# The first two units in the form of the later ones: gated linear attention and a gated feed-forward layer on one core

## The chip, the core and the metric

The kernel runs on one core of a Trainium2 chip. A core has five engines with a queue of its own each: TensorE for matrix products (PE in the rows; PEld are its weight loads, PEq its sequencer), VectorE (DVE), ScalarE (ACT), GpSimd (POOL) and SyncE (SP), which here issues nearly all transfers. An engine works through its queue in order, and engines wait for one another by semaphores. Matrix products land in PSUM, eight banks, from where VectorE or ScalarE bring them to SBUF. The metric is the device time of one execution in microseconds (us).

## The reference

```python
def _attn_ref(q, k, v, alpha):                      # (4, 8, 768, 48) each
    state = np.zeros((B, H, D, D))
    for t in range(S):
        state = alpha[:, :, t, :, None] * state + np.einsum('bhd,bhe->bhde', k[:, :, t], v[:, :, t])
        y[:, :, t] = np.einsum('bhd,bhde->bhe', q[:, :, t], state)
    return y

def _moe_ref(x, w_gate, w_val, w_out):              # x (3072, 384); weights 384x1536, 384x1536, 1536x384
    g = x @ w_gate
    silu = g * (1.0 / (1.0 + np.exp(-g)))
    return silu * (x @ w_val) @ w_out
```

x is the attention's y with its 8 heads of 48 side by side. The weights come as 64-bit floats.

## The kernel before

**Two streams of work share the engines.** The attention is cut into 16 units, each 192 tokens of one batch with all 8 heads (4 units to a batch); a unit is three chunks c of 64 tokens, and its heads stand as four pairs g, the even head of a pair (j = 0) on partitions 0 to 47 and the odd one on 64 to 111. The feed-forward runs in seven blocks of tokens with 12 steps f of 128 hidden columns each; block 0 needs units 0 and 1. Each weight piece (g, v or o of a step, 384 KB) is read from HBM once, in 20 groups (group 0 to 2 one piece, the others two), cut from 64 bits to a float32 in three steps (`w3v0`, `w3v1`, `w3v2` for group 3), rounded to a float16 (`w3a`) whose rest is a second float16 (`w3p`). A product is nine matmuls of 128x128 weights.

**A unit.** `p`, `T`, `ea`/`ek`/`cq` bring alpha, k and q in, turned on TensorE, for units 0 to 3. `G` (L501) is a scan over alpha from behind, `f` (L505, L508) one from the front, `mk` makes the scaled keys Gs and `q` the scaled queries X[:, 0]. `K.c` (L554) turns chunk c's keys on TensorE and `kc.c` (L558, L559) copies them to the tile K, one copy for each head of the pairs; for units 4 to 15 VectorE turns them instead (`kr`, L570). `S` makes the scores, `ma` (L695) masks them into X[:, 1], `ad.c` adds chunk c's k v product to the state, `de` (L724) scales the state for the next unit, `Y` makes the outputs from values, states and X, `yh` and `yl` (L803) round them to a pair of float16, `R` and `x` put them into the block's input. `vc` copies the values to a tile U. `z`, `ib`, `is`, `ik`, `im`, `iv` are fillings.

**Two forms.** For units 2 to 15, `scores_carry` interleaves scores (L623, diagonal quarters of the 128x128 array) with the k v products of the chunks (L631, the other two quarters), `advance` adds them chunk by chunk with two instructions, one for each j (L718), and `outputs_quarters` (L754) makes the outputs in quarters. Units 0 and 1 (u < NST) use `scores`, then `carry` (L673), whose products run over all 128 rows and bring all three states out at once, since values (64 rows) and state (48 rows, on the other half) stand in one tile V of 96 columns to a pair, and the keys in K the same way, with an identity in chunk 0's state rows; `advance` then only copies (L709, L716, on ScalarE); `outputs` (L767 to L784) likewise mixes values and state in one product for two of four pairs.

**What sets the order.** ORDER, a string of some 1450 words `engine:step@banks`, is the program: each word issues one step on the named engine (t TensorE, v VectorE, s ScalarE, g GpSimd, y the transfers on SyncE), and each engine's queue is the words with its letter. Nothing reorders it.

Of the kernel before, what the change touches and what calls it, by code (L numbers as in the profile page):

```python
# [31 lines left out]
NST = 2  # L32
# [115 lines left out]
def main_path(ctx, tc, q, k, v, alpha, w_gate, w_val, w_out, out, flag, spill):  # L148
# [52 lines left out]
    DV = 2 * D  # L201
    Vt = [cp.tile([P, NU, G, DV], F32, name=f"V{i}") for i in range(NV)]
# [5 lines left out]
    nc.vector.memset(Vt[0], 0.0)  # L208
# [24 lines left out]
    VC = (slice(0, D), slice(D, DV))  # L233


    KC = (slice(0, D), slice(D, 2 * D))
    KW = NU * G * 2 * D
    Kt_ = [cp.tile([P, KW + 16], F32, name=f"K{i}") for i in range(NK)]
    Kt = [t_[:, 0:KW].rearrange("p (c g x) -> p c g x", c=NU, g=G) for t_ in Kt_]

    def keys_made():
        for t_ in Kt_:
            nc.gpsimd.memset(t_, 0.0)
        for t_ in Kt:
            for j in range(2):
                r = slice(j * BO, j * BO + D)
                nc.gpsimd.tensor_copy(out=t_[r, 0, :, KC[j]], in_=ident[r, r].unsqueeze(1).to_broadcast([D, G, D]))

# [269 lines left out]
    def qhat(u, eng):  # L518
# [12 lines left out]
    def q_odd(u, eng):  # L531
        X, r = state[u]["X"], slice(BO, BO + D)
        (eng.copy if eng is nc.scalar else eng.tensor_copy)(out=X[r, 1, 0:GF, :], in_=X[r, 0, 0:GF, :])

    def values_copied(u, eng):

        Vd = state[u]["V"]
        g0 = 0 if u >= NST else GF
        for j, r in ((0, slice(BO, P)), (1, slice(0, BO))):
            (eng.copy if eng is nc.scalar else eng.tensor_copy)(  # L540
                out=U[j * BO : j * BO + C, :, g0 * D : G * D].rearrange("p c (g e) -> p c g e", e=D),
                in_=Vd[r, :, g0:, VC[j]],
            )
# [37 lines left out]
    def scores(u, banks):  # L581

        st = state[u]
        KTt, X = st["Gs"], st["X"]
        st["S"] = [ps.tile([P, 512], F32, tag=banks[f], name=f"s{f}_{u}") for f in range(2)]
        st["sps"] = [t_[:, 0 : GF * T].rearrange("p (g t) -> p g t", g=GF) for t_ in st["S"]]
        for c in range(NU):
            cs = slice(1 + c * C, 1 + (c + 1) * C)
            cx = slice(c * C, (c + 1) * C)
            for g0 in range(GF):  # L590
                for f in range(2):
                    g = f * GF + g0
                    for j in range(2):
                        r, o = slice(j * BO, j * BO + D), (j if f else 1 - j) * BO
                        nc.tensor.matmul(
                            st["sps"][f][o : o + C, g0, cx], KTt[r, g, cs], X[r, 0, g, cx], start=True, stop=True
                        )

    def scores_carry(u, banks):
# [793 lines left out]
```

## Time and profile before

| | us |
|---|---|
| median of 3 runs | 515.17 (515.12 to 516.37) |
| the profiled execution | 514.84, span 513.1 |
| TensorE busy | 497.9 (97% of the span) |
| VectorE, ScalarE, GpSimd busy | 371.0, 285.3, 136.0 |
| transfers | 71.17 MB, mean 139 GB/s |

The span runs from the first to the last instruction; 1.7 us of the execution lie around it. Until about 34.5 us the core prepares units 0 and 1 and the first weights; from there feed-forward products follow one another on TensorE, with the later units between them, until the last output rows.

### The profile page before, as it was taken

The page shows a single profiled execution, that of the slowest core. Times are in us where ns is not written, and L with a number is a line of the kernel's source. Part 1 is how long each engine was busy: PE and PEld are TensorE (multiplying, and loading weights), DVE is VectorE, ACT ScalarE, POOL GpSimd, SP SyncE. Part 2 cuts the span into 40 slices and gives each one's busy share as a digit, 9 for nine tenths or more (in the row PEclk, how much of TensorE's full clock was granted, in tenths as well). Part 3 has the DMA queues.
Part 4 walks back from the last instruction along what each step waited for, and adds up shares of the span by engine and source line. Part 5 has one row for each costly group of instructions (what it writes and reads, how often), then busy time and mean ns, then how long its engine had stood idle before and what let it go on. Part 6 is the DMA issues. An engine that isn't in the chain of part 4 may idle for free.

```text
span 513.1 us, 13634 instructions
## 1 busy us (share of the span) xinstructions
PE 497.9 (97%) x5439; PEld 288.2 (56%) x5439; DVE 371.0 (72%) x617; ACT 285.3 (56%) x630; POOL 136.0 (27%) x152
## 2 busy tenths in 40 slices
PE   4999999999999999999999999999999999999995
PEld 4876666566666666655455554544554545456663
DVE  5999999999979989996978858936768334123123
ACT  5998998326431723333544425425317965589982
POOL 7544342235234322414214122121203100001100
PEclk9999999999999999999999999999999999999999
DMA  8999585555546444555655253453353624363521
GB/s 213 273 261 320 173 265 145 123 139 139 161 110 173 116 100 111 142 146 133 160 129 139 62 142 77 111 135 72 86 137 79 170 69 126 101 176 86 147 47 53
DMA packets 115143, 71.17 MB, mean 139 GB/s; under 512 B 64384, under 2 KB 112000, under 8 KB 115072
## 3 DMA queue, kind: packets, MB, share of 16 engines
q1 hardware_dynamic: 114368, 69.49, 51.3%
q8 instruction: 44, 0.72, 0.6%
q10 hardware_dynamic: 704, 0.74, 0.5%
q14 instruction: 27, 0.22, 0.1%
HBM read 61.34 MB, written 4.72 MB: 129 GB/s over the span
## 4 chain that ended last, share of the span: by engine, by line
PE 89%; DVE 4%; issue 2%; ACT 2%; DMA 1%; POOL 1%; SPq 0%; DVEq 0%; ACTq 0%; POOLq 0%
PE v L871 26%; PE g L871 26%; PE ops L953 14%; PE ops L958 13%; PE y L754 4%; PE s L623 2%; PE pt L448 1%; PE A L631 1%; DMA raw<-in_moe_w_val_dram 1%; DVE t L136 1%; DVE Gs L501 1%; DVE w L362 1%; PE kps L554 0%; DVE Gs L1067 0%; DVE h L887 0%
## 5 line engine op out<-in xcount | busy, mean ns | idle before, releaser
L871 PEld LDWEIGHTS <-w 128*128 128x128 f16 x1530 | 147.7, 98 | 131.8 <-issue 2.0
L871 PE MATMUL v<-xT,w 128*128 128x384 f16 (+2 forms) x765 | 154.1, 347 | 1.1 <-DVE h L885 0.7
L871 PE MATMUL g<-xT,w 128*128 128x384 f16 (+2 forms) x765 | 154.1, 347 | 0.3 <-ACT h L879 0.3
L899 POOL TENSOR_TENSOR hl<-h,hh 128x384 f16<-128x384 f32 (+1 forms) x54 | 63.3, 1176 | 245.8 <-ACT hh L893 238.4
L893 ACT CAST hh<-h 128x384 f16<-128x384 f32 (+1 forms) x84 | 46.1, 553 | 83.2 <-DVE h L887 43.5
L879 ACT ACTIVATE h<-g 128x384 f32<-128x384 f32 (+1 forms) x84 | 44.5, 530 | 84.5 <-PE g L871 84.4
L958 PE MATMUL ops<-w,hh 128*128 128x384 f16 x286 | 75.8, 326 | 0.0
L887 DVE TENSOR_TENSOR h<-h,v 128x384 f32<-128x384 f32 (+1 forms) x63 | 38.2, 607 | 51.3 <-PE v L871 42.6
L953 PE MATMUL ops<-hh,w 128*128 128x512 f16 x216 | 69.3, 379 | 0.0
L570 DVE STREAM_TRANSPOSE K<-Gs 32x384 f32<-32x384 f32 x96 | 54.7, 570 | 1.9
L953 PEld LDWEIGHTS <-w 128*128 128x128 f16 x324 | 31.4, 98 | 37.3
L958 PE MATMUL ops<-w,hl 128*128 128x384 f16 x143 | 46.6, 326 | 0.0
L899 DVE TENSOR_TENSOR hl<-h,hh 128x512 f16<-128x512 f32 (+1 forms) x30 | 19.4, 647 | 29.9 <-ACT hh L893 29.8
L953 PE MATMUL ops<-hl,w 128*128 128x512 f16 x108 | 40.9, 379 | 0.0
L958 PEld LDWEIGHTS <-hh 128*128 128x128 f16 x286 | 28.0, 98 | 18.4
L501 DVE TENSOR_TENSOR_SCAN Gs<-AT,Z 128x776 f32<-128x776 f32 x16 | 28.5, 1782 | 4.6 <-ACT AT L1041 4.4
L68 ACT ACTIVATE X<-y 112x384 f16<-112x384 f32 x28 | 12.8, 488 | 32.1 <-PE y L754 27.2
L527 POOL TENSOR_TENSOR X<-trq,AT 112x768 f32<-112x768 f32 x11 | 18.7, 1701 | 45.2 <-DMA V<-in_v_dram 13.2
L508 DVE TENSOR_TENSOR_SCAN AT<-AT,Z 128x774 f32<-128x774 f32 x16 | 30.0, 1877 | 0.6
L885 DVE SCALAR_TENSOR_TENSOR h<-v,h 128x384 f32<-128x384 f32 (+1 forms) x21 | 12.9, 612 | 19.5 <-PE v L871 17.5
L1070 POOL TENSOR_TENSOR Gs<-trk,Gs 128x768 f32<-128x768 f32 x10 | 16.8, 1683 | 32.5 <-DVE trk L423 32.4
L327 ACT ACTIVATE wc<-wc,wbias 128x384 f32<-128x384 f32 x36 | 23.4, 651 | 1.2
(155 smaller groups left out, 688.7 us busy)
## 6 DMA issues: line engine op xcount, KB each, us to landing
raw<-in_moe_w_gate_dram SPq DMA_DIRECT2D x12, 384.0 KB, 5.2
V<-in_v_dram SPq DMA_DIRECT2D x96, 48.0 KB, 3.6
raw<-in_moe_w_val_dram SPq DMA_DIRECT2D x12, 384.0 KB, 6.2
raw<-in_moe_w_out_dram SPq DMA_DIRECT2D x12, 384.0 KB, 5.9
wc<-in_moe_w_gate_dram SPq DMA_DIRECT2D x12, 384.0 KB, 4.1
wc<-in_moe_w_out_dram SPq DMA_DIRECT2D x12, 384.0 KB, 3.8
wc<-in_moe_w_val_dram SPq DMA_DIRECT2D x12, 384.0 KB, 3.8
L<-in_k_dram SPq DMA_DIRECT2D x24, 144.0 KB, 2.9
```

The lines of the kernel that those rows point to most:

```text
L327: nc.scalar.activation(dev, dev, AF.Relu, bias=wbias[:, 1:2], accum_out=wviol[:, 0, i : i + 1])
L501: nc.vector.tensor_tensor_scan(Gf[:, ::-1], Af[:, ::-1], Z[:, : 0 : -1], 0.0, op0=ALU.mult, op1=ALU.add)
L508: nc.vector.tensor_tensor_scan(Af, Af, Z[:, 1 : n + 1], Z[:, 0:1], op0=ALU.mult, op1=ALU.add)
L570: nc.vector.transpose(out=bass.AP(k0.tensor, k0.offset, [k0.ap[0], (G * 2 * D, NU), (2 * D, G), (1, 32)]), in_=Kg[j * BO + x : j * BO + x ...
L754: nc.tensor.matmul(to, w_, x_, start=(m == 0), stop=(m == 1))
L871: nc.tensor.matmul(pt, wsp[kind, f][a][:, kt * P : (kt + 1) * P], xT[blk][:, b_, kt, cs], start=(n == 0), stop=(n == 3 * KT - 1),)
L879: nc.scalar.activation(h, acc.pop(("g", blk, f)), AF.Silu, scale=(-1.0 if ("g", f) in negative else 1.0) / H_SCALE)
L887: nc.vector.tensor_tensor(out=h, in0=h, in1=v_, op=ALU.mult)
L893: (eng.copy if eng is nc.scalar else eng.tensor_copy)(out=hh, in_=acc["h", blk, f])
L899: eng.tensor_tensor(out=hl, in0=acc.pop(("h", blk, f)), in1=hh, op=ALU.subtract)
L953: nc.tensor.matmul(ops[blk][i], wsp["o", f][a][:, i * P : (i + 1) * P], h[b_], start=(first and n == 0), stop=(last and n == 2),)
L958: nc.tensor.matmul(ops[blk][i], h[b_][:, i * P : (i + 1) * P], wsp["o", f][a], start=(first and n == 0), stop=(last and n == 2),)
```

## The change

ORDER is new in its first third and the same, word for word, in its last 990 words. The special form of units 0 and 1 goes: `scores`, `carry`, `outputs`, `q_odd` and NST are deleted, and `scores_carry` and `outputs_quarters` serve all units. States get tiles St of their own, 112 rows by 48 columns to a pair, with the even head's state on rows 0 to 47 and the odd one's on 64 to 111, and V keeps only values, 48 columns to a pair. With this one instruction of 112 rows in `advance` and `decay` covers both heads of the pairs, in all units. K has 64 columns to a pair (48 of keys, 16 zeros), so that the k v product writes all 64 rows of a half. `k_turned` turns keys by eight plain products with the identity in two quarters of the array, instead of four transposes of 112 rows, and one copy brings them to K.

```diff
     def k_turned(u, c, bank):
-        kps = state[u]["kps", c] = ps.tile([C, G, 112], F32, tag=bank, name=f"kps{u}_{c}")
+        kps = state[u]["kps", c] = ps.tile([P, G, D], F32, tag=bank, name=f"kps{u}_{c}")
+        cs = slice(1 + c * C, 1 + (c + 1) * C)
         for g in range(G):
-            cs = slice(1 + c * C, 1 + (c + 1) * C)
-            nc.tensor.transpose(kps[:, g, :], state[u]["Gs"][0:112, g, cs], ident[0:112, 0:112])
+            for j in range(2):
+                r = slice(j * BO, j * BO + D)
+                nc.tensor.matmul(
+                    kps[(1 - j) * BO : (2 - j) * BO, g, :], state[u]["Gs"][r, g, cs], ident[r, r], start=True, stop=True
+                )
     def k_copied(u, c):
...
-        nc.scalar.copy(out=Ks[BO : BO + C, c, :, KC[0]], in_=kps[:, :, 0:D])
-        nc.scalar.copy(out=Ks[0:C, c, :, KC[1]], in_=kps[:, :, BO : BO + D])
+        nc.scalar.copy(out=Ks[:, c, :, 0:D], in_=kps)
...
-                            to[j * BO : j * BO + D], Ks[r, c, g, KC[j]], Vd[r, c, g, VC[j]], start=True, stop=True
+                            to[j * BO : (j + 1) * BO], Ks[r, c, g, :], Vd[r, c, g, :], start=True, stop=True
...
+    def advance(u, c, eng):
+
+        r, Sd = slice(0, 112), St[u % NV]
+        for gs, cps in state[u]["cps"][c]:
+            to = Sd[r, c + 1, gs] if c + 1 < NU else SE[r, gs]
+            if c == 0 and first_of_batch(u):
+                (eng.copy if eng is nc.scalar else eng.tensor_copy)(out=to, in_=cps[r])
+            else:
+                eng.tensor_tensor(out=to, in0=cps[r], in1=Sd[r, c, gs], op=ALU.add)
...
-                                w_, x_ = Vd[r, c, g, j * D : j * D + k], X[r, 0, g, cx]
+                                w_, x_ = Sd[r, c, g, :], X[r, 0, g, cx]
...
-        todo[f"S{u}"] = lambda eng, *banks: (scores if u < NST else scores_carry)(u, banks)
...
+        todo[f"S{u}"] = lambda eng, *banks: scores_carry(u, banks)
+        todo[f"Y{u}"] = lambda eng, *banks: outputs_quarters(u, banks)
```

In ORDER, beside this: the loads of unit 1's alpha and unit 0's q stand ahead of weight group 0's; unit 1's `q` moves from GpSimd to VectorE, two of the tile copies `p` and the second cutting steps of groups 1 to 4 from GpSimd to ScalarE, group 0's from ScalarE to GpSimd; the state additions of units 0 and 1 are new on VectorE but for the first, a copy on ScalarE.

VectorE's queue from unit 0's last masking to unit 1's first, before (Gs are keys, X queries and masked scores, s scores, SE the state at a unit's end, w and t weights, Y outputs, raw weights as loaded, pt a turned input; the digit behind a name is the unit, the group, or the half and the unit):

```order
L695 TENSOR_TENSOR X0_106<-s1_0_242,mask_104 128x384
L70 TENSOR_SCALAR w0_346<-t0_179 128x384
L695 TENSOR_TENSOR X0_106<-s0_0_241,mask_104 64x384 x2
L362 SCALAR_TENSOR_TENSOR w0_346<-t0_179,w0_346 128x384
L724 SCALAR_TENSOR_TENSOR V1_90<-SE_110,Gs1_274 48x4x48 x2
L136 SCALAR_TENSOR_TENSOR t1_343<-raw1_217,t1_343 128x384
L501 SCALAR_TENSOR_TENSOR Gs2_483<-AT_96,Z_87 128x776
L695 TENSOR_TENSOR X1_107<-s1_1_393,mask_104 128x384
```

The same place in VectorE's queue with the change (S are the states, A the k v products, trq the turned queries):

```order
L623 TENSOR_TENSOR S0_91<-A2_0_282,S0_91 112x192
L609 TENSOR_TENSOR X0_108<-s1_0_281,mask_106 128x384
L519 TENSOR_TENSOR X1_109<-trq1_337,AT_98 112x768
L623 TENSOR_TENSOR SE_112<-A2_0_282,S0_91 112x96
L623 TENSOR_TENSOR SE_112<-A3_0_283,S0_91 112x96
L69 TENSOR_SCALAR w0_388<-t0_203 128x384
L609 TENSOR_TENSOR X0_108<-s0_0_280,mask_106 128x384
L355 SCALAR_TENSOR_TENSOR w0_388<-t0_203,w0_388 128x384
L628 SCALAR_TENSOR_TENSOR S1_92<-SE_112,Gs1_276 112x192
L493 SCALAR_TENSOR_TENSOR Gs2_512<-AT_98,Z_87 128x776
L623 TENSOR_TENSOR S1_92<-A2_1_462,S1_92 112x192
```

Three additions and unit 1's q have come in, one masking instruction of two and one of two decays have gone, and group 1's cutting step stands further back.

VectorE's queue about unit 3's keys (Gs3), before (h are hidden values):

```order
L362 SCALAR_TENSOR_TENSOR w3_676<-t3_478,w3_676 128x768
L501 SCALAR_TENSOR_TENSOR Gs3_723<-AT_96,Z_87 128x776
L887 TENSOR_TENSOR h0_0_721<-h0_0_721,v0_0_693 128x384
L1067 TENSOR_TENSOR Gs3_723<-pt3_1_0_741,Gs3_723 128x4x32x3
L1067 TENSOR_TENSOR Gs3_723<-pt3_1_1_745,Gs3_723 128x4x32x3
L362 SCALAR_TENSOR_TENSOR w4_719<-t4_649,w4_719 128x768
L136 SCALAR_TENSOR_TENSOR t5_725<-raw5_611,t5_725 128x768
```

And with the change:

```order
L355 SCALAR_TENSOR_TENSOR w4_731<-t4_686,w4_731 128x768
L761 TENSOR_TENSOR h0_0_733<-h0_0_733,v0_0_706 128x384
L135 SCALAR_TENSOR_TENSOR t5_720<-raw5_514,t5_720 128x768
L493 SCALAR_TENSOR_TENSOR Gs3_798<-AT_98,Z_87 128x776
L940 TENSOR_TENSOR Gs3_798<-pt3_1_0_785,Gs3_798 128x4x32x3
L940 TENSOR_TENSOR Gs3_798<-pt3_1_1_789,Gs3_798 128x4x32x3
L628 SCALAR_TENSOR_TENSOR S0_91<-SE_112,Gs2_512 112x192
```

The rest of group 4 and a cutting step of group 5 now stand ahead of unit 3's keys, and unit 2's decay behind them. On TensorE the two turnings of unit 3's keys (`K3.1`, `K3.2`) have moved the other way: before, they follow products g2, S2, v2 and g3; now they stand right behind g2:

```order
L745 MATMUL g0_2_802<-xT0_599,w4_731 128x384
L543 MATMUL kps3_1_822<-ident_101,Gs3_798 64x48 x8
L543 MATMUL kps3_2_841<-ident_101,Gs3_798 64x48 x8
L594 MATMUL s0_2_853<-X0_108,Gs2_512 64x64 x2
L602 MATMUL A2_2_855<-V0_89,K0_110 64x48 x2
```

S2, v2, g3 and v3 come behind the turnings; up to v3's start both programs have issued the same steps on TensorE, in another order.

## Rows read from the trace of the kernel before

**Rows 1.** The page, busy us of each engine, share of the span, instructions

```profile
PE 497.9 (97%) x5439; PEld 288.2 (56%) x5439; DVE 371.0 (72%) x617; ACT 285.3 (56%) x630; POOL 136.0 (27%) x152
```

**Rows 2.** Stretches: length, busy us (count) PE, PEld, DVE, ACT, POOL; PEclk, DMA, GB/s

```profile
6.80:34.56 27.76, 24.50 (x460) 21.01 (x461) 26.32 (x38) 23.87 (x57) 14.73 (x20) 1.00 1.03 291
34.56:60.00 25.44, 25.09 (x268) 17.69 (x266) 25.05 (x41) 22.75 (x41) 9.98 (x10) 1.00 0.80 231
60.00:100.00 40.00, 39.60 (x489) 25.10 (x487) 38.96 (x52) 31.16 (x50) 11.10 (x12) 1.00 0.63 181
100.00:220.00 120.00, 119.35 (x1576) 75.42 (x1574) 108.74 (x177) 49.05 (x119) 42.02 (x38) 1.00 0.51 132
```

**Rows 3.** TensorE's timeline: start, us, line, tile, count [idle before]

```profile
42.50 1.63 PE L871 MATMUL g<-xT,w 128*128 128x384 f16 x9
...
47.07 1.63 PE L871 MATMUL g<-xT,w 128*128 128x384 f16 x9
48.53 0.93 PE L554 MATMUL kps<-ident,Gs 112*64 112x112 f32 x8
49.82 1.62 PE L871 MATMUL v<-xT,w 128*128 128x384 f16 x9 [0.35 <-DVE h L885]
```

**Rows 4.** Who waited for whom: us in total, times, longest

```profile
PE v L871 <- DVE h L885: 0.7, 2, 0.4
PE v L871 <- DVE h L887: 0.4, 1, 0.4
```

**Rows 5.** VectorE's timeline to 58 us

```profile
6.80 1.77 DVE L501 TENSOR_TENSOR_SCAN Gs<-AT,Z 128x776 f32<-128x776 f32 x1 [3.76 <-ACT AT L1041]
13.91 1.77 DVE L501 TENSOR_TENSOR_SCAN Gs<-AT,Z 128x776 f32<-128x776 f32 x1 [0.61 <-ACT AT L1041]
15.79 0.96 DVE L1070 TENSOR_TENSOR Gs<-trk,Gs 128x768 f32<-128x768 f32 x1
19.45 1.14 DVE L695 TENSOR_TENSOR X<-s,mask 64x384 f32<-64x384 f32 x2
20.51 1.45 DVE L362 SCALAR_TENSOR_TENSOR w<-t,w 128x384 f16<-128x384 f32 x1
21.88 0.73 DVE L724 SCALAR_TENSOR_TENSOR V<-SE,Gs 48x192 f32<-48x192 f32 x2
33.33 1.01 DVE L362 SCALAR_TENSOR_TENSOR w<-t,w 128x384 f16<-128x384 f32 x2
36.49 1.41 DVE L136 SCALAR_TENSOR_TENSOR t<-raw,t 128x768 uint32<-128x768 uint32 x1
40.83 1.02 DVE L1067 TENSOR_TENSOR Gs<-pt,Gs 128x384 f32<-128x384 f32 x2
46.15 0.95 DVE L136 SCALAR_TENSOR_TENSOR t<-raw,t 128x768 uint32<-128x768 uint32 x1
48.35 0.95 DVE L362 SCALAR_TENSOR_TENSOR w<-t,w 128x768 f16<-128x768 f32 x1
49.69 0.73 DVE L718 TENSOR_TENSOR V<-A,V 48x192 f32<-48x192 f32 x2
56.08 1.07 DVE L718 TENSOR_TENSOR SE<-A,V 48x96 f32<-48x96 f32 x4
```

**Rows 6.** ScalarE's timeline in the same stretch

```profile
15.93 0.31 ACT L558 COPY K<-kps 64x192 f32<-64x192 f32 x1 [0.26 <-PE kps L554]
```

**Rows 7.** GpSimd's timeline in the same stretch

```profile
19.86 1.69 POOL L527 TENSOR_TENSOR X<-trq,AT 112x768 f32<-112x768 f32 x1
36.06 1.03 POOL L436 COPY wide<-L 128x576 f32<-128x576 f32 x1
```

**Rows 8.** Lines of TensorE and its weight loads: count, busy us, mean ns

```profile
L623 PEld LDWEIGHTS s<-X,Gs 48*64 48x64 f32 x672 | 20.7, 134 | 5.1 <-issue 4.7 <-POOL hl L899 0.4
L631 PEld LDWEIGHTS A<-V,K 64*48 64x48 f32 x536 | 15.8, 119 | 0.0
```

**Rows 9.** Weight loads in time, unit 0's scores alone

```profile
14.45 0.79 PEld L595 LDWEIGHTS s<-X,Gs 48*64 48x64 f32 x48 [0.30 <-issue]
```

More of the change, by code (lines that the diff above doesn't have):

```diff
@@ L31 @@
 NPE = 4
-NST = 2
 NHALVED = 7
@@ L200, in main_path @@
     nc.vector.memset(Z, 0.0)
-    DV = 2 * D
-    Vt = [cp.tile([P, NU, G, DV], F32, name=f"V{i}") for i in range(NV)]
+    Vt = [cp.tile([P, NU, G, D], F32, name=f"V{i}") for i in range(NV)]
+    St = [cp.tile([P, NU, G, D], F32, name=f"S{i}") for i in range(NV)]
     NP = 2
@@ L207, in main_path @@
         nc.gpsimd.memset(x[:, :, :, D:].rearrange("p j e x -> p (j e) x"), 1.0)
-    nc.vector.memset(Vt[0], 0.0)
+    nc.vector.memset(St[0][:, 0], 0.0)
     AT = cp.tile([P, G, T2], F32, name="AT")
@@ L232, in main_path @@
     Xt = [cp.tile([P, 2, G, T], F32, name=f"X{i}") for i in range(NX)]
[L233 to L239, printed above, removed]
+    KW = NU * G * BO
+    Kt_ = [cp.tile([P, KW], F32, name=f"K{i}") for i in range(NK)]
+    Kt = [t_.rearrange("p (c g x) -> p c g x", c=NU, g=G) for t_ in Kt_]
     def keys_made():
-        for t_ in Kt_:
-            nc.gpsimd.memset(t_, 0.0)
         for t_ in Kt:
-            for j in range(2):
-                r = slice(j * BO, j * BO + D)
-                nc.gpsimd.tensor_copy(out=t_[r, 0, :, KC[j]], in_=ident[r, r].unsqueeze(1).to_broadcast([D, G, D]))
+            nc.gpsimd.memset(t_[:, :, :, D:], 0.0)
     SE = cp.tile([P, G, D], F32, name="SE")
@@ L529, in qhat @@
             )
-    def q_odd(u, eng):
-        X, r = state[u]["X"], slice(BO, BO + D)
-        (eng.copy if eng is nc.scalar else eng.tensor_copy)(out=X[r, 1, 0:GF, :], in_=X[r, 0, 0:GF, :])
     def values_copied(u, eng):
         Vd = state[u]["V"]
-        g0 = 0 if u >= NST else GF
         for j, r in ((0, slice(BO, P)), (1, slice(0, BO))):
             (eng.copy if eng is nc.scalar else eng.tensor_copy)(
-                out=U[j * BO : j * BO + C, :, g0 * D : G * D].rearrange("p c (g e) -> p c g e", e=D),
-                in_=Vd[r, :, g0:, VC[j]],
+                out=U[j * BO : j * BO + C, :, 0 : G * D].rearrange("p c (g e) -> p c g e", e=D),
+                in_=Vd[r],
             )
@@ L568, in k_rows @@
             r = (1 - j) * BO + y
-            k0 = Kt_[u % NK][r : r + 32, j * D + x : j * D + x + 32]
+            k0 = Kt_[u % NK][r : r + 32, x : x + 32]
             nc.vector.transpose(
-                out=bass.AP(k0.tensor, k0.offset, [k0.ap[0], (G * 2 * D, NU), (2 * D, G), (1, 32)]),
+                out=bass.AP(k0.tensor, k0.offset, [k0.ap[0], (G * BO, NU), (BO, G), (1, 32)]),
                 in_=Kg[j * BO + x : j * BO + x + 32, :, :, y : y + 32],
@@ L579, in first_of_batch @@
         return units[u][1] == 0
[L581 to L597, printed above, removed]
     def scores_carry(u, banks):
@@ L699, in causal @@
         )
     def advance(u, c, eng):
-        st = state[u]
-        Vd = st["V"]
-        if st["whole"] and c < 2:
-            for j in range(2 * c):
-                r = slice(j * BO, j * BO + D)
-                eng.copy(out=Vd[r, 2:0:-1, :, VC[j]], in_=st["cps10"][r])
-            return
-        for gs, cps in st["cps"][c]:
-            for j in range(2):
-                r = slice(j * BO, j * BO + D)
-                to = Vd[r, c + 1, gs, VC[j]] if c + 1 < NU else SE[r, gs]
-                if st["whole"] or c == 0 and first_of_batch(u):
-                    (eng.copy if eng is nc.scalar else eng.tensor_copy)(out=to, in_=cps[r])
-                else:
-                    eng.tensor_tensor(out=to, in0=cps[r], in1=Vd[r, c, gs, VC[j]], op=ALU.add)
@@ L720, in decay @@
-    def decay(u, eng):
-        for j in range(2):
-            r = slice(j * BO, j * BO + D)
-            eng.scalar_tensor_tensor(
-                out=Vt[u % NV][r, 0, :, VC[j]], in0=SE[r], scalar=1.0 / FRAME,
-                in1=state[u]["Gs"][r, :, 0:1].to_broadcast([D, G, D]), op0=ALU.mult, op1=ALU.mult,
-            )
+        r, Sd = slice(0, 112), St[u % NV]
[5 more added lines that the diff above has]
+                eng.tensor_tensor(out=to, in0=cps[r], in1=Sd[r, c, gs], op=ALU.add)
@@ L789, in rows_of @@
         if "Y" not in st:
-            st["Y"] = st["X"].bitcast(F16) if u >= NST else p2.tile(
+            st["Y"] = st["X"].bitcast(F16) if u >= 2 else p2.tile(
                 [112, 2, G, T], F16, tag=f"w{len(wgroups) - 2 - u}", name=f"Y{u}", bufs=1
```

118 lines of the change are left out of this document (18 added, 100 removed).

## The prediction, as put on record

> **What bounds the kernel now.** I read the page first: TensorE is busy for 97% of the span and nothing else comes near [rows 1]. Then the busy time by stretches [rows 2]: from 34.56 us on TensorE has almost no gap (0.35 us to 60 us, 0.40 to 100 us, 0.65 to 220 us), while before that it serves the preparation. So a change of this kind moves the end in three ways only: the products start earlier, they get longer or shorter, or their gaps do. The same rows show what the first two stretches hang on: VectorE is busy for 26.32 of 27.76 us, 25.05 of 25.44 us and 38.96 of 40 us. From the first scan at 6.80 us [rows 5] to about 100 us it has 3% to spare, and the rest of the kernel 10% and more. The third view, who TensorE waits for, agrees: of its waits behind 34 us, 1.1 us are for hidden values h, which VectorE makes [rows 4]. The start is VectorE's, not TensorE's, so I sum up VectorE's queue.
>
> **The change part by part.**
>
> *VectorE's queue up to unit 3's keys.* I take the end of `mk3`, at 40.83 + 1.02 = 41.85 us [rows 5], as the mark, because with the change TensorE wants it at once: K3.1 and K3.2 now stand right behind product g2. What leaves the queue ahead of that mark: one masking instruction each for units 0 and 1, 2 x 0.57 (half of 1.14); half of unit 0's decay, 0.37; unit 2's decay, which moves behind, 0.73. Sum 2.2 us. What comes in: three additions of 192 columns, each half of the pair of 0.73, 0.37 x 3 = 1.1; four of 96 columns, 1.07 for the four; unit 1's q from GpSimd, which is the two-tensor form of 128x768 at 0.96; and the rest of group 4 (0.95) with group 5's cutting step (0.95), which move ahead of `mk3`. Sum 5.0 us. Net +2.8 us [all rows 5].
>
> *What the queue loses in waits and collisions.* The rest of a group of 384 columns took 1.45 us at 20.51, while GpSimd made unit 1's q (19.86 to 21.55), and two of them took 1.01 at 33.33; a cutting step took 1.41 us at 36.49, beside a GpSimd copy from 36.06, and 0.95 at 46.15 [rows 5, 7]. With q and that copy off GpSimd this gives back 0.95 + 0.46 = 1.4 us. [...]
>
> Unit 1's scan G1 stood 0.61 us waiting for ScalarE's alpha copy [rows 5]; unit 1's turning no longer stands behind unit 0's keys, but the copy still waits for unit 0's q, which `f0` now precedes: I take 0.3 of the 0.6. Against it a new wait: `ad1.0` stands in the queue until TensorE has done S1, which starts when Y0 ends, which needs unit 0's last masking. From there VectorE has w0's rest, a decay and a scan ahead of `ad1.0`, about 0.5 + 0.37 + 1.77 = 2.6 us, and TensorE two blocks of about 1.55 us: 0.5 us of waiting, between 0 and 3.1, and behind it stand the outputs' rounding, unit 2's keys and all weight groups. Together: 41.85 + 2.8 - 1.4 - 0.3 + 0.5 = 43.4 us. Added up from each instruction's undisturbed length instead, the queue comes to 42.5. I take 43.0, with 42.2 and 43.9 as ends.
>
> *TensorE around the mark.* Before, g2 starts at 42.50, and S2, v2 and g3 end at 48.53, with 1.46 a product (47.07 to 48.53): the block of S2, v2 and g3 is 48.53 - 42.50 - 1.46 = 4.57 us [rows 3]. With the change K3.1 starts at 43.05, the two turnings take 0.93 as before, and v3 starts at 43.05 + 0.93 + 4.57 = 48.55, against 49.82: **1.3 us earlier**, with the wait of 0.35 in front of v3 [rows 3] in that sum. That TensorE is there in time hangs on unit 1's part of the block's input. Its last rounding loses the scan `f2` in front of it (1.9 us, now behind), so I put it near 31.4 us, the packing's end near 33, g2's end near 42; TensorE then stands about 1 us for unit 3's keys. If the keys were ready, v3 would start at 42.0 + 5.5 = 47.5, and no earlier.
>
> *Behind the mark.* VectorE's list up to the last weight group loses, after `mk3`: for units 2 and 3 half of each pair of additions, 4 x 0.37, half of the four of 96 columns, 0.53, and half of unit 3's decay, 0.37; one rounding of a weight group net, about 0.4; and the 1.9 us that moved ahead; it gains unit 2's decay, 0.37 [rows 5]. That is 4.3 us less. `mk3` ends 1.15 us later than before, so VectorE reaches the last group some 3 us earlier, and products ask for it only 1.3 us earlier. Two of the three waits for h are left (1.1 - 0.35 = 0.75 us, rows 3 and 4); I take half of them as gone, **0.4 us**. For units 4 to 15 the additions are halved too, about 1.6 us of VectorE a unit, and there it buys nothing: VectorE has 11 us free from 100 to 220 [rows 2].
>
> *Edits that cost or bring nothing by themselves.* ScalarE loses one of two key copies, 0.31 us, twelve times [rows 6], and the copies of states, and takes over two tile copies and four cutting steps: a relief of some us that TensorE does not see, since the engine is not full (23.87 of 27.76 us, rows 2). GpSimd's filling of K and V shrinks, off the path. Smaller tiles move no transfer. Loads: weight group 0 lands about 0.6 us later, behind unit 1's alpha and before unit 0's q is worked off; VectorE's first use of it now comes behind f0.
>
> *Keys turned in quarters.* No row shows a turning by plain products. Eight products are 16 passes, two quarters at a time; unit 0's 48 passes of scores, four quarters at a time, go by at (0.79 - 0.13) / 47 = 14 ns [rows 9], so a quarter needs 56 ns: 8 x 56 = 0.45 us, and 0.9 if the quarters took turns. Now a chunk takes 0.93 / 2 = 0.47 [rows 3]. I take no difference; only unit 3's three chunks stand among products, so the upper end is 3 x 0.43 = 1.3 us.
>
> Sum: 1.3 + 0.4 = 1.7 us, from the profiled execution's 514.84 to 513.1. That execution lies 0.3 under the median of the three runs, so for a median I say 513.3.
>
> **The rivals.**
>
> *VectorE keeps it.* `mk3` ends at 43.9 or later, because the additions wait for S0 and S1 longer than I think or collide with GpSimd's value copies, one such collision having cost 0.95 us [rows 5]. Then v3 starts at 49.4, 0.4 us is left and the later waits stay: 514.4. For it speaks that VectorE is the bound and gets 5.0 us of new work ahead of the mark; against it that GpSimd has half of its work there no more.
>
> *The keys are ready.* `mk3` ends by 41.95, v3 starts at 47.5, all waits for h go: 2.35 + 0.75 = 3.1 us, 511.7. It needs 0.5 us less than the sum of undisturbed lengths.
>
> *Wider weights make it slower.* The k v products of units 2 to 15 now load 64 columns instead of 48. Loads of 64 columns take 134 ns, of 48 columns 119 [rows 8]. If loads set the pace of the block of scores and k v products, it grows as the columns do, 128 to 112 for a pair: 1.55 / 7 = 0.22 us, 14 times, 3.1 us, nothing to hide them in a full TensorE, and the kernel ends at 516.2. It decides where the passes of four quarters no longer cover the loads. Against it: the scores alone, all with 64 columns, went by at 14 ns a pass [rows 9], no slower than the mixed block, 1.55 / 96 = 16 ns. [...]
>
> **How the numbers follow.** The forecast, 512.6 to 513.9 for a median, has 52%; VectorE keeping it 27%; the keys ready 12%; the wider weights 9%. About 0.3%, 1.55 us, is what a measurement of this kernel can tell from no change. Faster by more than that: 12% and four fifths of the forecast, 53%; within it: the rest of the forecast, the 27% and 2% of the last, 40%; slower 7%. The range reaches from the keys' case (511.9 for a median) past the first rival's 514.7 to 515.3, and leaves out most of the last.
>
> **What would show it.** Right: unit 3's keys end near 43 us in VectorE's timeline, TensorE shows about 1 us of waiting for Gs in front of the turning behind g2, v3 starts near 48.5, the block of scores and k v products still takes 1.55 us, and the waits for h shrink. Wrong: additions that wait over 1 us for A, a block of 1.7 us or more, key turnings near 0.9 us each, or products that stand for weights near 34 us, which my sum does not have.

## The result: slower by 1.45%, and the profile after

The changed kernel takes 523.18 us (median of 4 runs, 521.82 to 524.08) against 515.46 us of the kernel before beside it (515.12 to 516.37): a ratio of 1.0145, interval 1.0114 to 1.0176. The forecast was 513.3 us, and the range ended at 515.3. The profiled execution took 524.04 us, its span is 522.3. The line of the page that answers to [rows 1]:

```profile
PE 502.8 (96%) x5599; PEld 292.0 (56%) x5599; DVE 347.0 (66%) x567; ACT 279.8 (54%) x609; POOL 117.3 (22%) x135
```

VectorE has lost 24 us of work, as the change meant it to, and the profiled execution is 9 us longer. The stretches of [rows 2], read from the trace after, tell where:

```profile
6.80:34.56 27.76, 20.04 (x505) 17.49 (x509) 21.82 (x36) 16.20 (x33) 5.12 (x10) 0.89 0.95 291
34.56:60.00 25.44, 25.44 (x324) 18.79 (x317) 19.25 (x32) 20.39 (x37) 5.12 (x5) 0.78 0.63 184
60.00:100.00 40.00, 40.00 (x505) 25.76 (x504) 36.39 (x49) 33.12 (x51) 12.21 (x13) 1.00 0.64 186
100.00:220.00 120.00, 119.79 (x1550) 75.73 (x1552) 102.97 (x157) 48.21 (x115) 34.46 (x31) 1.00 0.51 132
```

VectorE, full before, now stands for 6 us of the first stretch and 6 of the second; in the first the others stand too, TensorE for 7.7 us. No engine is full up to 34.56 us. And the granted clock, 1.00 in every stretch before, is 0.89 and 0.78. (The record of the clock begins at 14.4 us in the trace before and at 15.0 in the one after; what lies ahead of that counts as 1.00.) The same columns over the pieces in which the clock was one or the other:

```profile
14.00:21.80 7.80, 6.16 (x175) 5.39 (x175) 6.31 (x7) 5.20 (x14) 1.88 (x3) 1.00 0.90 269
21.80:25.20 3.40, 3.40 (x64) 3.07 (x67) 3.35 (x8) 2.31 (x7) 0.00 (x0) 0.50 0.96 317
25.20:32.00 6.80, 4.17 (x199) 3.63 (x192) 3.31 (x9) 5.41 (x10) 1.99 (x3) 1.00 1.06 380
32.00:45.70 13.70, 13.19 (x160) 9.91 (x161) 8.16 (x16) 7.25 (x15) 0.00 (x0) 0.50 0.83 231
45.70:60.00 14.30, 14.30 (x218) 10.72 (x216) 13.65 (x23) 13.66 (x24) 5.12 (x5) 1.00 0.45 136
```

TensorE ran for 17 us (3.4 and 13.7) at the lower of the two levels in that record, 0.50. Ahead of each fall it stood, for 1.45 and 1.71 us. TensorE's timeline (start, us, line, tile, count, and in brackets the idle time ahead and what ended it):

```profile
11.27 2.79 PE L441 MATMUL pt<-ident,wide 128*128 128x128 f32 x12 [2.35 <-DVE Gs L940]
14.00 2.02 PE L543 MATMUL kps<-ident,Gs 48*64 48x48 f32 x48
...
21.03 0.67 PE L543 MATMUL kps<-ident,Gs 48*64 48x48 f32 x16 [1.45 <-DVE X L609]
...
27.55 0.27 PE L594 MATMUL s<-X,Gs 48*64 48x64 f32 x2 [0.82 <-issue]
...
31.45 0.24 PE L658 MATMUL y<-X,U 64*64 64x64 f32 x1 [1.71 <-DVE Gs L940]
...
33.63 0.34 PE L658 MATMUL y<-X,U 64*48 64x64 f32 x2 [0.43 <-issue]
...
58.78 1.46 PE L745 MATMUL v<-xT,w 128*128 128x384 f16 x8
```

Three of the stands are for a PSUM bank that VectorE has to read out first. Tq0 (11.27) goes into a bank of Tk0, which `mk0` frees, and `mk0` now stands behind `f0`. K1.2 (21.03) goes into a bank of the scores, which the masking `ma0.2` frees, now behind an addition. Y1 (31.45) goes into the banks of Tk2, which `mk2` frees. The other two are for nothing that the profile names; I come to them below. The last row is v3, at 58.78 where the prediction had 48.55 and the kernel before 49.82 [rows 3]. VectorE's own timeline shows the other side: an addition that waits for S1, a cutting step that waits for ScalarE, and unit 3's keys, which end at 52.72 us where the prediction had 43.0:

```profile
29.03 0.36 DVE L623 TENSOR_TENSOR S<-A,S 112x192 f32<-112x192 f32 x1 [3.49 <-PE A L602]
...
44.68 0.96 DVE L135 SCALAR_TENSOR_TENSOR t<-raw,t 128x768 uint32<-128x768 uint32 x1 [4.27 <-ACT t L119]
...
51.69 1.03 DVE L940 TENSOR_TENSOR Gs<-pt,Gs 128x384 f32<-128x384 f32 x2 [0.34 <-PE pt L441]
```

For the rest I use one mark, the start of ScalarE's first activation, `sl0`: 38.69 us before, 47.04 after, 8.35 us later. So nearly the whole loss is there by 47 us. v3, the prediction's own mark, is 8.96 us later; activation 36 stands 7.78 us later than before, so behind v3 the change gains 1.2 us. From activation 16 to 36, while the scores of units 5 to 9 go by, the distance goes from 8.05 to 7.78 (7.98 from 20 to 32) and does not grow, so a unit's blocks cost what they cost before. At 291.17 us, in unit 10's outputs, TensorE stands once more for nothing named, and the distance comes to 9.5:

```profile
291.17 0.21 PE L658 MATMUL y<-X,S 48*48 48x64 f32 x1 [1.37 <-issue]
```

### The profile page after: what moved, and what is told of

It reads as the page before. It is cut to its first block, busy times and chain, and to the rows that moved or that the text cites. A ratio compares the mean times of both kernels' runs of the same rounds, so it can differ in the third digit from the quotient of the medians.

```text
span 522.3 us, 13849 instructions
## 1 busy us (share of the span) xinstructions
PE 502.8 (96%) x5599; PEld 292.0 (56%) x5599; DVE 347.0 (66%) x567; ACT 279.8 (54%) x609; POOL 117.3 (22%) x135
## 4 chain that ended last, share of the span: by engine, by line
PE 89%; DVE 4%; DMA 3%; issue 1%; ACT 1%; SPq 1%; POOL 1%; DVEq 0%; POOLq 0%
PE g L745 25%; PE v L745 25%; PE ops L827 13%; PE ops L832 12%; PE y L658 4%; PE s L594 3%; PE pt L441 2%; PE kps L543 2%; DMA raw<-in_moe_w_gate_dram 1%; DMA raw<-in_moe_w_out_dram 1%; PE A L602 1%; DVE t L135 1%; PE xp L710 1%; DVE Gs L493 1%; DVE w L355 1%
## 5 line engine op out<-in xcount | busy, mean ns | idle before, releaser
L773 POOL TENSOR_TENSOR hl<-h,hh 128x384 f16<-128x384 f32 (+1 forms) x53 | 61.1, 1156 | 261.4 <-ACT hh L767 245.8
L761 DVE TENSOR_TENSOR h<-h,v 128x384 f32<-128x384 f32 (+1 forms) x70 | 42.5, 608 | 68.3 <-PE v L745 64.3
L827 PEld LDWEIGHTS <-w 128*128 128x128 f16 x324 | 31.4, 98 | 37.3
L658 PE MATMUL y<-X,U 64*48 64x64 f32 (+1 forms) x768 | 27.6, 225 | 2.3 <-DVE Gs L940 1.7
L658 PE MATMUL y<-X,S 48*48 48x64 f32 x768 | 28.3, 223 | 1.4 <-issue 1.4
L658 PEld LDWEIGHTS y<-X,U 64*64 64x64 f32 (+1 forms) x768 | 24.7, 131 | 7.7 <-issue 5.1
L594 PEld LDWEIGHTS s<-X,Gs 48*64 48x64 f32 x768 | 23.8, 134 | 5.9 <-issue 5.9
```

The costliest lines, as they stand in the source:

```text
L594: nc.tensor.matmul(st["sps"][g // GF][j * BO : j * BO + C, g % GF, cx], KTt[r, g, cs], X[r, 0, g, cx], start=True, stop=True,)
L658: nc.tensor.matmul(to, w_, x_, start=(m == 0), stop=(m == 1))
L761: nc.vector.tensor_tensor(out=h, in0=h, in1=v_, op=ALU.mult)
L773: eng.tensor_tensor(out=hl, in0=acc.pop(("h", blk, f)), in1=hh, op=ALU.subtract)
L827: nc.tensor.matmul(ops[blk][i], wsp["o", f][a][:, i * P : (i + 1) * P], h[b_], start=(first and n == 0), stop=(last and n == 2),)
```

## The experiments

The executions of one kernel with the change scatter by up to 6 us; so a profile explains its own execution, and comparisons rest on medians and ratios.

| run | us, median | ratio to before, interval | `sl0` in its profile, us |
|---|---|---|---|
| again | 523.86 | 1.0183, 1.0166 to 1.0200 | 44.66 |
| fill | 521.30 | 1.0114, 1.0095 to 1.0133 | 46.03 |
| unblock | 523.17 | 1.0179, 1.0133 to 1.0225 | 44.11 |
| stand | 518.71 | 1.0086, 1.0068 to 1.0105 | 42.90 |
| mkfirst | 520.08 | 1.0116, 1.0099 to 1.0133 | 41.23 |
| both | 520.09 | 1.0119, 1.0091 to 1.0147 | 42.54 |
| ffirst | 516.39 | 1.0034, 1.0020 to 1.0048 | 40.75 |
| best | 519.65 | 1.0100, 1.0084 to 1.0117 | 43.58 |
| codegap | 523.72 | 1.0158, 1.0138 to 1.0177 | 47.66 |
| new | 519.70 | 1.0093, 1.0076 to 1.0110 | 41.97 |
| turn_after | 520.88 | 1.0113, 1.0090 to 1.0137 | 45.33 |
| turn_new | 518.36 | 1.0063, 1.0047 to 1.0078 | 41.97 |
| late_new | 518.06 | 1.0069, 1.0053 to 1.0085 | 41.11 |
| late_mk | 518.67 | 1.0071, 1.0047 to 1.0096 | 43.36 |

### What the clock is worth: again, fill, stand

> The changed kernel once more, for a second profile. Theory A (the halved clock): what it loses over the kernel before is mostly TensorE running at its lower level, 17.1 us of the first 46; where this profile shows fewer us at the lower level, the time should fall by about half of the difference, so that without any it would be near 515. Theory B (the waits themselves): the 3.2 us that TensorE stands for banks, and VectorE's 3.5 us for the products of unit 1, push every later step back; the time stays at 520 to 522 whatever the clock shows.

Its profile is of an execution of 520.61 us, a time that theory B allows too. The stands at 8.8 us, at K1.2 and at Y1 are the same (2.35, 1.45 and 1.70 us); the clock is not. Its record begins at 19.9 us there, and what it was before I take from the pace: unit 0's turnings take 2.80 us, where they took 2.02 in the first profile, and the records of unit 0's scores go from 0.31 to 0.22 us at 19.9. Behind that one stretch of 6.8 us:

```profile
13.91 2.80 PE L543 MATMUL kps<-ident,Gs 48*64 48x48 f32 x48
```

```profile
23.30:30.10 6.80, 6.80 (x183) 6.47 (x184) 3.83 (x8) 4.76 (x11) 0.67 (x2) 0.50 1.02 342
```

Counted from 15 us on, with 4.9 us by the pace and 6.8 by the record, TensorE is at the lower level for some 12 us against 17, and `sl0` stands at 44.66 against 47.04: 5 us less, 2.4 us earlier. That is about half, as theory A has it, though the first profile also stands for 0.82 us in S1 and this one does not. The four executions of `unblock` say the same: with mean granted clocks of 0.997, 0.994, 0.987 and 0.985 over the span they took 519.9, 521.0, 525.3 and 525.8 us. By my estimate 0.012 of 519 us is 12.5 us at 0.50, and the time differs by 5.9, again about half. Not all executions say so: those of `mkfirst`, with 0.995, 0.990, 0.985 and 0.994, took 517.5, 520.1, 520.1 and 521.3 us. And the slope of the four of `unblock` ends at 518 to 519 us where theory A had 515, so the clock is not all.

`fill` adds 13 products on the identity in the two long waits:

```diff
-t:K1.2@7 ... t:Y1@20
+t:fA@6 t:K1.2@7 ... t:fB@7 t:Y1@20
```

> The changed kernel with throwaway products of 128x128 on TensorE in its two long waits: 6 ahead of K1.2, 7 ahead of Y1, each into a bank that is free there. The waits for VectorE stay as they are. Theory A: the granted clock stays at 1.00 from 15 us on, the first product g0.0 starts near 39 instead of 43.6 and the time is 516 to 518.5. Theory B: the clock may rise but g0.0 stays behind VectorE's late steps, within 1.5 us of 43.6, and the time is 520.5 to 522.5.

It came out as theory B had it: 521.3 us, and g0.0 starts at 42.64, within 1.5 us of 43.6. Theory A's condition, the clock at 1.00 from 15 us on, was not met: the full pace came at 19.6 us, and the clock fell again for 3.4 us at 29.8, behind a stand of 2.62 us in S1, where no filler lies. The fillers themselves take 3.5 us of TensorE (1.60 and 1.88), so the run does not separate the clock from their own cost.

`stand` goes the other way: one wait in the kernel before.

```diff
-v:f2 (behind Y1 in the program)  t:Y1@20
+v:f2 t:st@2 t:Y1@20
+    todo["st"] = lambda eng, bank: nc.tensor.matmul(ps.tile([1, 1], F32, tag=bank, name="stand"), AT[:, 0, 0:1], AT[:, 0, 0:1], start=True, stop=True)
```

> The kernel before with one wait added: ahead of Y1, TensorE does a product of one element that reads what f2 writes, so that it stands from about 29.2 to 31.5 us (2.3 us); nothing of VectorE's queue changes. Theory A: the granted clock falls to the lower level behind the stand and stays there for some 10 us, so the time grows by 2.3 us and 4 to 6 more: 521 to 523.5. Theory B: the clock plays no part, the time grows by 2.3 us at most: 515.5 to 517.5.

518.71 us, between the two. The wait is there, and as it ends the clock falls, for 6.8 us:

```profile
31.46 0.19 PE L1194 MATMUL stand<-AT 128*1 128x1 f32 x2 [2.18 <-DVE AT L508]
```

```profile
31.10:37.90 6.80, 6.38 (x87) 5.08 (x88) 3.56 (x8) 2.36 (x7) 0.00 (x0) 0.50 0.92 234
```

2.2 us of standing and half of 6.8 are 5.6; the time grew by 3.95 us, since some of it took the place of later waits (0.38 us at 33.11 and 0.35 in front of v3 are gone). So a wait of 2 us on TensorE cost the old kernel 4. How these divide between the wait and the clock is not shown: the execution of 518.25 us had a mean clock of 0.993, the one of 520.41 us 0.995.

### What the order is worth: mkfirst, ffirst, unblock, both, best

`mkfirst` undoes one exchange of two words; `ffirst` makes the same exchange in the kernel before.

```diff
-v:f0 v:mk0
+v:mk0 v:f0
```

> The changed kernel with mk0 ahead of f0 again on VectorE, as in the kernel before, and nothing else. It frees the bank of Tq0 2 us earlier, so that TensorE's stand at 8.9 us falls from 2.35 to about 0.9. In the profiles so far the turnings of units 0 and 1 ran at the lower pace until 15 us in one and until 20 us in three of the four kernels with the change, until 14 us in both with the old start. Theory A (the clock's rise hangs on that stand): full pace from 14 to 15 us, S0 starts near 16.5 instead of 18 to 19.5, and the time falls to 517 to 520.5. Theory C (the rise is chance or hangs on something later): full pace as late as 20 us still, time 521 to 523.5.

> The kernel before with f0 ahead of mk0 on VectorE, the one edit of the new order that costs TensorE its stand at 8.9 us. Theory A: the stand grows from 0.86 to about 2.3 us, the pace rises at 14 us or later, up to 20, and the time grows by 1.5 to 4 us, 516 to 519. Theory D (VectorE bounds the start, as the prediction had it, and f0 costs the same in front or behind): 514.3 to 515.5.

Both came out as theory A had them. 520.08 us against 523.86 and 523.18: 3.4 us by the ratio of `again`, 1.5 by that of the first result, whose interval overlaps with this one's. The full pace is there from 12.2 us on, and the clock falls once, at 25.9 us for 3.4. In the kernel before, the exchange costs 1.85 us, and the clock, up from 16.2 us on, stays up; from `sl0` on the whole program is shifted by some 2.06 us. The stand ahead of TensorE's next transposes, of mkfirst and then of ffirst:

```profile
9.50 2.82 PE L441 MATMUL pt<-ident,wide 128*128 128x128 f32 x12 [0.68 <-ACT wide L429]
```

```profile
11.64 0.96 PE L554 MATMUL kps<-ident,Gs 112*64 112x112 f32 x4 [2.78 <-DVE Gs L1067]
```

`unblock` takes the waits at K1.2 and Y1 away:

```diff
-v:ad0.1 v:ma0.2   t:Tk2@02   v:ad1.0 v:yl0.1 v:ma1.0 v:mk2 v:ad1.1 v:ma1.2 ... v:yl0.0
+v:ma0.2 v:ad0.1   t:Tk2@37   v:yl0.1 v:yl0.0 v:ad1.0 v:ma1.0 v:ma1.2 v:mk2 v:ad1.1
```

> The changed kernel with the waits taken away at their root, by order and banks alone: unit 0's second masking stands ahead of its second state addition (it frees the bank of K1.2), unit 0's roundings stand in VectorE's empty time ahead of unit 1's first addition, and unit 2's keys are turned into the banks of unit 0's outputs, so that Y1 no longer waits for mk2. Both theories expect TensorE's waits at K1.2 and Y1 to fall from 1.45 and 1.71 us to about 0.7 and 0.6. Theory A: if the granted clock stays at 1.00 with it, 514 to 516; if it still falls, 519 to 521. Theory B: 519.5 to 521 in either case, the 2 us of the waits and no more.

The waits went as wanted, to 0.73 us and to under 0.3. The time did not: 523.17, above what either theory gave. TensorE now stands inside S1, for nothing the profile names, and longer:

```profile
29.95 0.27 PE L594 MATMUL s<-X,Gs 48*64 48x64 f32 x2 [3.16 <-issue]
```

> The changed kernel with mk0 ahead of f0 and with the order and banks of the unblocking run together. Theory A: full pace from 14 to 15 us and at most one short stretch at the lower clock behind it, 515 to 518. Theory B (VectorE's and ScalarE's later steps set the start of the products whatever TensorE does): 518.5 to 521.

With both edits 520.09, in theory B's range and no better than mkfirst alone; K1.2 and Y1 no longer wait over 1 us for VectorE, and 1.95 us of standing has moved into Y1.

> As the run before the last, and VectorE's queue arranged for TensorE: mk1 and unit 0's second masking stand ahead of f1, its first masking and the additions ahead of unit 1's q, and two cutting steps of weight groups stand in VectorE's empty time ahead of unit 1's additions. Theory A: K1.2 no longer waits over 0.5 us, the clock stays up from 15 us on and the time is 513.5 to 516. If TensorE still stands for its instructions near 27 us (2 to 3 us, as in two of the last profiles) and drops its clock behind it, 516 to 519.

519.65, above both ranges, and with a miss of mine in it: K1.0 waited 2.97 us for `ea2`, which stood behind a cutting step of weights on ScalarE.

### What TensorE stands for when nothing is named: codegap, new, turn_new, turn_after, late_new, late_mk

The page's third part lists a DMA queue that carries instructions, in the changed kernel with 46 packets and 0.75 MB, so 16 KB each:

```profile
q8 instruction: 46, 0.75, 0.6%
```

Set beside the stands that "issue" ended (one was put down to an engine long done), these transfers give a pattern. The first column counts TensorE's records in the trace, weight loads, products and the few of its sequencer, from the start of the program, and names the first one behind the stand:

| kernel, record | reached, us | transfer starts | goes on | after its start |
|---|---|---|---|---|
| before, 706 | 27.59 | 24.96 | 27.85 | 2.89 |
| after, 706 | 26.73 | 25.09 | 27.55 | 2.46 |
| after, 962 | 33.20 | 31.40 | 33.63 | 2.23 |
| fill, 706 | 26.63 | 26.79 | 29.25 | 2.46 |
| unblock, 706 | 26.79 | 27.70 | 29.95 | 2.25 |
| mkfirst, 706 | 23.29 | 23.19 | 25.60 | 2.41 |
| both, 962 | 28.56 | 28.12 | 30.51 | 2.39 |
| new, 706 | 23.22 | 23.00 | 25.31 | 2.31 |
| new, 962 | 29.36 | 29.24 | 31.67 | 2.43 |
| turn_after, 706 | 26.83 | 28.25 | 30.62 | 2.37 |

Whatever the order, TensorE stopped in these ten rows at the same numbers, 256 apart, whichever step lies there, and went on 2.2 to 2.9 us after a transfer of 16 KB had begun. I had not seen that in the profile of before, though its 0.26 us in unit 1's carry is the same thing. The stand at 291.17 us is of the same kind: it is record 7362, 26 x 256 behind 706, and 2.18 us after a transfer's start. Every kernel with the change has one near there (7362, or 7106 where the keys are turned by four transposes), of 0.45 to 1.5 us, but `fill`: its 52 records of fillers put other products at that number, and there the distance to before is 6.7 us at activation 36 and at the last. In all 16 profiles, with places and transfers counted off against each other, no place was passed sooner than 2.18 us after the start of its transfer. That TensorE waits for these transfers is argued from this; no run changed them alone.

`codegap` puts Tk2 between Y0 and S1, on top of mkfirst:

```diff
-t:Y0@37 ... t:S1@4651 ... t:Tk2@02    s:w1v0 ... s:ea2 ... s:pk2
+t:Y0@37 ... t:Tk2@02 t:S1@4651        s:ea2 s:pk2 s:w1v0
```

> The run with mk0 ahead of f0, and beside it unit 2's key turning Tk2 put between Y0 and S1 (ScalarE widens those keys earlier for it). In the profiles so far TensorE stands at the same place of its code, 705 instructions on, inside S1, when it gets there less than 2.3 us after the start of a 16 KB transfer of its own instructions, and Y0 and S1 bring it there within 2.4 to 3 us of the 256 instructions before. Theory E (TensorE outruns its instructions): the 0.9 us of Tk2 in front of S1 takes as much off that stand (2.31 us in the run before), Y1's wait for mk2 (1.05 us) goes to below 0.4 too, and the time falls by 1 to 2 us against 520.1: 518 to 519.3. Theory F (the stand is for data, unit 1's values or keys): the stand keeps its end and its size changes by less than 0.3 us with Tk2 behind it in time, 519.5 to 521.

Inconclusive: the stand in S1 shrank to under 0.3 us, as E wanted, but in that execution TensorE came there late, after 3.4 us at the lower clock in turnings and Y0 (22.4 to 25.8 us), and Y1's wait grew, since `mk2` stands behind an addition that waits for the later S1. 523.72 us, outside both.

```profile
32.15 0.24 PE L658 MATMUL y<-X,U 64*64 64x64 f32 x1 [2.50 <-DVE Gs L940]
```

`new`, on top of mkfirst, gives every turning a free bank and VectorE an order for TensorE (ScalarE's queue is moved to match):

```diff
-t:K1.2@7 t:Ta2@60 t:K1.1@1 t:K1.0@6 t:Y0@37 t:S1@4651 t:Tk2@02 t:Y1@20 t:R0.2@7 t:K2.0@5 t:K2.1@4
+t:K1.2@1 t:K1.1@6 t:Ta2@04 t:K1.0@7 t:Y0@32 t:Tk2@07 t:S1@4651 t:K2.0@3 t:K2.1@2 t:Y1@70 t:R0.2@4 t:K2.2@6
-v:G2 v:ad1.0 v:yl0.1 v:ma1.0 v:mk2
+v:G2 v:mk2 v:yl0.1 v:yl0.0 v:ad1.0 v:ma1.0 v:ma1.2
```

> The same with banks chosen so that no turning waits for a masking: K1.2 and K1.1 go into banks that are free when S0 ends, unit 2's keys are made and turned between S1 and Y1, and VectorE does mk2 and unit 0's roundings ahead of unit 1's additions. All of the changed functions stay. If TensorE's stands and its clock are what the new order lost, the profile shows no stand over 1 us behind 9 us but for instructions, at most 3.4 us at the lower clock behind 15 us, and the time is 513 to 516. If TensorE outruns its instructions all the more, now that nothing else holds it, the stands for them grow to 3 us and more and it stays at 516 to 518.

The first part came true for the banks, and with it the last: TensorE waits for no bank over 0.6 us, and stands 4.4 us for instructions. It did not for the clock, which was at the lower level for 6.8 us behind 15 us, not 3.4 at most.

```profile
18.12 1.13 PE L543 MATMUL kps<-ident,Gs 48*64 48x48 f32 x32 [0.53 <-DVE Gs L943]
25.31 0.37 PE L594 MATMUL s<-X,Gs 48*64 48x64 f32 x1 [2.09 <-issue]
31.67 0.25 PE L658 MATMUL y<-X,S 48*48 48x64 f32 x1 [2.30 <-issue]
```

The median, 519.70 us, is above the 516 to 518 that I had for it. Then the turning in quarters was undone, in the changed kernel and in `new`:

```diff
-    kps[(1 - j) * BO : (2 - j) * BO, g, :], state[u]["Gs"][r, g, cs], ident[r, r], ...
+    nc.tensor.transpose(kps[:, g, :], state[u]["Gs"][0:112, g, cs], ident[0:112, 0:112])
...
+        nc.scalar.copy(out=Ks[BO : BO + C, c, :, 0:D], in_=kps[:, :, 0:D])
+        nc.scalar.copy(out=Ks[0:C, c, :, 0:D], in_=kps[:, :, BO : BO + D])
```

> The changed kernel with its keys turned as before: four transposes of 112 rows and two copies to K for each chunk; the tiles, the order and all else stay as changed. In the profiles with the change a chunk's turning takes 16 matmuls and 0.67 us at the full clock, before 4 matmuls and 0.48 us; with the weight loads that is 24 instructions a chunk fewer, 216 for the nine chunks ahead of the first product. Theory E (TensorE outruns its instructions, and the change made them more): the stands for instructions before 35 us, 1.3 us in the changed kernel's profile, go or move, TensorE also stands less for its turnings, 1 to 2 us, and the time falls by 2 to 4.5 us to 519 to 521.5. Theory G (the turning costs only its own time, in a stretch full of other waits): within 1.5 us of the changed kernel, 522 to 524.

> The run with banks chosen so that no turning waits (4.4 us of stands for instructions, 519.7) with the four transposes and two copies in place of the turning in quarters. Theory E: the 216 instructions fewer ahead of the first product are nearly one of the 16 KB transfers, the two stands of 2.1 and 2.3 us shrink to less than half together, the turnings take 9 x 0.2 us less, and the time falls to 515 to 517.5. Theory G: the stands keep their size at other places, the time falls by the 1.8 us of the turnings at most, 518 to 519.5.

turn_after fell to 520.88 us, in E's range, but not in E's way: its stand for instructions is the longest of all, 3.79 us. turn_new fell by 1.3 us to 518.36, which is G's, and its stands are 1.77 and 2.25 us where E wanted less than half of 4.4. So E falls in this form: fewer instructions move work across the places, the stands stay. But the turning in quarters has a price: undone, it gives back 1.3 us in `new` and 2.3 to 3.0 in the changed kernel, by the medians. Last, the loads of weight groups 4 to 7 were to go behind Y1, in turn_new and in mkfirst:

```diff
-y:wl4 ... y:wl5 ... y:wl7 ... y:wl6 ... t:Y1
+t:Y1 y:wl4 y:wl5 y:wl7 y:wl6
```

> The run with free banks and transposes (518.4 us, stands for instructions of 1.77 and 2.25 us), with the loads of weight groups 4 to 7, four groups of up to two pieces, issued behind Y1 instead of between S0 and Y1. In the profiles a weight transfer issued at 20 to 28 us lands 5 to 8 us later, behind others, and the instruction transfers start 1 to 3.7 us after TensorE enters the stretch of 256 instructions ahead of them. Theory H (instruction transfers queue behind the weights): the transfers start at least 1 us sooner, the two stands fall below 2 us together, and the time is 515.5 to 517.5 unless the later weights are then waited for. Theory I (TensorE reaches these places too early whatever the weights do): both stands stay within 0.7 us of their size and the time is 518 to 519, or more if the weights come late.

> The same move of the loads of groups 4 to 7 in the run with mk0 ahead of f0 alone (520.1 us; a stand of 2.31 us for instructions in S1). Theory H: that stand falls below 1.3 us and the time to 518 to 519.3. Theory I: it stays at 1.7 to 3 us and the time at 519.5 to 521.

The edit did not do what it was made for. Nothing ties SyncE's queue to Y1, so the loads only moved behind those of unit 3's alpha and keys: SyncE issues them from 21.40 to 27.55 us in late_new where it was 20.16 to 26.57, and from 20.81 to 26.09 in late_mk where it was 20.39 to 27.66, all ahead of Y1's first product (28.68 and 28.40). So neither theory was tested, though the medians, 518.06 and 518.67 us, fall in I's and in H's range. In late_mk the stand fell from 2.31 to 1.23 us; in late_new both stayed, 2.05 and 2.21; and whether the transfers wait behind the weights is open. But late_new answers something else: its clock is at 1.00 from 12.5 us to the end of the products, and it has no wait for a bank over 1 us.

```profile
27.14 0.27 PE L591 MATMUL s<-X,Gs 48*64 48x64 f32 x2 [2.05 <-issue]
...
34.92 0.71 PE L441 MATMUL pt<-ident,wide 128*128 128x128 f32 x5 [2.21 <-issue]
```

```profile
14.00:35.00 21.00, 14.03 (x436) 11.33 (x437) 17.00 (x31) 17.51 (x42) 4.77 (x6) 1.00 0.98 301
```

Its profiled execution took 517.26 us, the fastest of its six, `sl0` at 41.11, 2.4 us later than before, with 4.3 us of stands for instructions and 2.1 us of waits for ScalarE's tile copies ahead of it. No version that I ran beats the kernel before. What late_new still loses, 3.4 us by the medians, is not taken apart: no run with the change is without stands for instructions, and none has the new functions in the old order, so what each of the two costs or gains is not known beyond the key turning.

## Why the prediction was wrong, by its own steps

**"The start is VectorE's, not TensorE's."** This step failed. It holds for the kernel before as it was ordered: VectorE is full there [rows 2]. I summed VectorE's queue and let TensorE follow. In the new order TensorE waits at three places for a bank and not for data, 5.5 us in the first profile, and I walked VectorE's queue for data alone. After the change VectorE stands 12 us in 53, and unit 3's keys end at 52.72 us, not 43.0. Of the three waits the first is shown to cost time, by the exchange of `mk0` and `f0`; with the other two gone (`unblock`) the time stayed, and stands for instructions and the lower clock were there in their place.

**The edit at no cost.** I knew that `f0` now precedes unit 0's keys and q, and looked only at what it does to VectorE and to ScalarE's alpha copy. With it Tq0 waits 2.35 us, without it 0.68 (mkfirst). Undone it gives back 1.5 to 3.4 us, done alone it costs 1.85.

**"0.5 us of waiting, between 0 and 3.1"** for unit 1's first addition. 3.49 us, above the upper end. S1 did not follow Y0 at the pace of rows at full clock: K1.2's stand of 1.45 us and 3.4 us at the lower clock came first, then 0.8 us for instructions.

**The end of 43.9 us** for unit 3's keys was to cover that GpSimd's value copies cost their neighbours on VectorE something. No run shows that cost: in the changed kernel's profile unit 0's copies ran from 18.81 to 20.64 us, and unit 1's keys and the first addition beside them took 0.93 and 0.36 us, no more than the 0.96 and 0.37 of my sum; unit 1's copies, from 26.60 to 27.98 us, fell into VectorE's stand.

**"TensorE is there in time."** Unit 1's last rounding was to end near 31.4 us and ended at 37.06 (35.92 and 1.14 on VectorE); v3 came at 58.78, not 48.55.

**The clock had no step at all.** Every stretch of before shows 1.00, and I took it for a constant. In the changed kernel it fell behind stands of 1.45 and 1.71 us, in `stand` with one of 2.18. It does not always: in late_new stands of 2.05 and 2.21 us passed without a fall. What decides it stays open.

**What held.** The block of scores and k v products costs no more with 64 columns: the distance to the kernel before is 8.05 us at activation 16 and 7.78 at activation 36, where the rival would have added five times 0.22. The rival of wider weights is refuted. The additions of 112x192 take 0.35 to 0.36 us, as priced. The gain behind the mark has the right sign but was too small: I had 0.4 us, and from v3 to activation 36 it is 1.1 to 1.2 us in all kernels with the change, where TensorE waits for h no more. The stand for instructions near 290 us, which my sum does not have, takes part or all of it back in every one but `fill`.

**"I take no difference"** for keys turned in quarters. A turning takes 1.13 us for two chunks (new) against 0.93 [rows 3]: 0.1 us a chunk more, inside my upper end of 0.43. But I counted only unit 3's chunks, and undoing the form gave back 1.3 to 3.0 us, at or above the 1.3 that I had for the worst case.

**The rival on the other side** had the right sign for the wrong reason. None of mine had TensorE stand for a bank or for instructions, or its clock fall. Of the signs of being wrong that I named, one came: an addition that waits over 1 us for A.

## What to carry to other kernels

When an order of queues is rewritten, follow each engine's waits for free buffers as well as for data: write down, for every PSUM bank that is used again, which instruction frees it and what now stands in front of that one. A wait of TensorE can cost more than its length: in `stand` one of 2.2 us, behind which the clock fell, cost 4. And an engine that shows no slack may only be full because the others serve it: VectorE, full in the kernel before, stood with the change for 6 of the 27.76 us from 6.80 us on.

## What the runs showed of the hardware

- In the ten stands of the table TensorE stood at places of its own instruction stream that lie 256 records apart, until 2.2 to 2.9 us after a 16 KB transfer of instructions had started; the 256 records ahead of 706 took 2.9 us in the changed kernel (23.88 to 26.73 us), so it was there 1.64 us after the transfer's start, and stood for 0.82. What starts the transfers, and why 1.2 to 3.9 us after the place before was passed in the rows of the table, stays open.
- The clock's rise at the start, by TensorE's pace and the beginning of the record, moved between 11 and 20 us among executions and kernels that differ little. With `mk0` first it came by 12.2 us in the first two profiles (mkfirst, both; stands of 0.68 and 0.48 us at 8.9 us), but at 17.3 and 18.9 us in those of best and codegap (0.48 and 0.82 us), so that stand is not all that decides it.
